# A planner that counts one more wait, and four pieces of work moved between queues, in a fused attention and gated-MLP block

## The chip, the cores and the metric

The kernel runs on one core of a Trainium2 chip. The metric is the device time of one execution in microseconds. A core has five engines that run their own instruction streams in order and meet at semaphores: TensorE (PE, matrix products into PSUM banks), VectorE (DVE), ScalarE (ACT), GpSimd (POOL) and SyncE (SP). A transfer (DMA) is issued by an instruction in the stream of an engine; in this kernel nearly all are issued by SP.

## What is computed

The input is x with 2048 rows of 576 columns. It is normalised row by row, goes through a 32-head attention (heads of 18 columns) and through a gated MLP of width 4608, and the two results are combined.

```
xn = layernorm(x)
q, k, v = split(xn @ wqkv)                       # 32 heads of 18
s = softmax(q @ k.T * 18 ** -0.5) @ v @ wo       # all heads, then the projection
h = gelu(xn @ w_gate) * (xn @ w_up)              # 2048 x 4608
g = silu(h @ w_down)
out = x + s * g
```

## The kernel before

**Numbers.** All large products are made of float16 matrices with a high and a low half (`whi`, `wlo`; `evh`, `evl`; `hhi`, `hlo`), three products for one. Weights are scaled by powers of two that come from their largest element, so each weight tile goes through a preparation: load (`raw`, and `draw` for the rows of `w_down`), row maxima on DVE (`amax`), a round trip through DRAM that spreads the maximum to all partitions (`mxd`, `mb`, then `top` on DVE), small scale operations, and the splits (`split_hi` on ACT, `split_lo` on GpSimd). `prep` (L211) returns these steps as a list of pieces. A `Rest(n)` among them holds the rest of the list back until n microseconds of planned time have passed.

**Stages.** First comes the layer norm, sixteen row tiles (`ln_scale` on DVE, `ln_hi` on ACT, `ln_lo` on GpSimd, transposes on PE), with q and k of the first six heads. Then, while PE works on v and on the q and k of the other heads in four groups j = 1 to 4, pair 0's score maxima begin. The results of a group leave PSUM by `evac_j` (L561): ACT writes the high half `evh`, DVE the low half `evl`, and `store` writes them to the DRAM tiles `QD[j]` and `KD[j]`, in six transfers for each block of 512 columns (four of `evh`, two of `evl`). `evh` and `evl` have three buffers each. Two rows of constants, `KD<-cst`, are added to each `KD[j]` by four transfers in `open_j` (L608).

**The main loop.** Attention runs over 16 pairs of heads. A step of it has a score product for the softmax (`qk2`, PE, then the exponential on ACT) and a score product of the next pair of heads for its row maxima (`qk1`, PE, then a `TENSOR_REDUCE` into `PM` on DVE). One PSUM tile each serves `qk1` and `qk2` here, so a step's products wait for the reduction and the exponential of the step before. Into a step go also slots of a gate/up product (two matrix products each, 27 slots to a unit) and stages D of the down projection. Two stages D make one output tile `y`; the first begins it in PSUM tile `md`, the second, called late, is followed on DVE by the addition into `y`, which frees `md`. A round is some six or seven steps, holds one gate/up unit, and ends with a closing step that has no slots but a burst: the products of the probabilities with v (L1498), into `md` or `ma`, then an addition into `osb` on DVE.

**What sets the order.** `make_plan` (L1701) chooses for each round how many steps it has, which of them hold a stage D and how many slots each one gets. It takes the cheapest by `lost` (L1680), a small model of PE, ACT and DVE with the constants of L1657 (slot 0.2158, stage D 0.735, the two score products 0.43, burst 2.9). In that model a stage D waits for the last addition into `y`; a burst does not. Other work (preparations, the softmax's normalisation, the gate's polynomial) is put between by `subtick` (L152) where the planned room of its engine allows.

**Around the end of a pair.** `max_end` (L1425) turns the row maxima into two extra rows of `QT`, in three parts a, b, c at three steps: a reduction (a), two small operations that make high and low halves `rmc` (b), a 32x32 transpose into `rms` and the transfers to DRAM and back into `QT` (c). All its arithmetic is on DVE. At the start of a pair `load_v` (L1406) loads its values `VT`.

Of the kernel before, what the change touches and what calls it, by code (L numbers as in the profile page):

```python
# [12 lines left out]
F32 = mybir.dt.float32  # L13
# [7 lines left out]
P = 128  # L21
# [74 lines left out]
def kernel(ctx: ExitStack, tc: tile.TileContext, x, wqkv, wo, w_gate, w_up, w_down, out):  # L96
# [114 lines left out]
    def prep(name, parts, n, down=None, urgent=False, free=None, dfree=None, lead=1, vec=(), spare=False, home=None, early=False, slow=1.0):  # L211
# [9 lines left out]
        def load():  # L221
            if spare:
                if spare == "P":
                    body = ap.tile([P, 2, 512], F32, tag="P", name=f"rawa_{name}", bufs=6)
                else:
                    body = wp.tile([P, 2, D], F32, tag="draw", name=f"rawa_{name}", bufs=1)
                body = body.rearrange("p a b -> p (a b)")[:, 0:8 * n].rearrange("p (t i n) -> p t i n", t=4, i=2)
                last = ap.tile([P, 512], F32, tag="osb", name=f"rawb_{name}", bufs=2)
                last = last[:, 0:2 * n].rearrange("p (i n) -> p i n", i=2)
            else:  # L230
                raw = wp.tile([P, 5, 2, n], F32, tag="raw", name=f"raw_{name}", bufs=1)
                body, last = raw[:, 0:4], raw[:, 4]
            w.raw = [body[:, t] for t in range(4)] + [last]
            (src, c0), (src1, c1) = parts
            rows = src.tensor.shape[1]
            if src1.tensor.name == src.tensor.name and c1 == c0 + n:
                cols = [(
                    [[1, 2 * n]], body.rearrange("p t i n -> p t (i n)"), last.rearrange("p i n -> p (i n)"), c0, src
                )]
            else:  # L240
                cols = [([[1, n]], body[:, :, i, :], last[:, i, :], c, t) for i, (t, c) in enumerate(parts)]
            for dims, dst, dst4, c, t in cols:
                q.dma_start(
                    dst,
                    bass.AP(tensor=t.tensor, offset=t.offset + c, ap=[[rows, P], [P * rows, 4]] + dims),
                )
                q.dma_start(
                    dst4,
                    bass.AP(
                        tensor=t.tensor, offset=t.offset + c + 512 * rows, ap=[[0, 2], [rows, 64]] + dims  # L250
                    ),
                )
# [147 lines left out]
        if early and down is not None:  # L400
            add(dload)
            rest(6.0)
        elif not early:
            rest(13.0)
        for t in range(5):
            add(lambda t=t: amax(t), dve)
        if down is not None:
# [153 lines left out]
    def evac_j(j, part, sb, mt, n, late=None):  # L561

        nh = n // DH
        ev = {}

        def hi():
            ev["h"] = wp.tile([P, 512], F16, tag="evh", name=f"evh_{j}_{part}_{sb}", bufs=3)
            nc.scalar.activation(ev["h"][0:n], mt.t[0:n], AF.Copy, scale=2.0 ** -22)
            mt.done()

        def lo():
            ev["l"] = wp.tile([P, 512], F16, tag="evl", name=f"evl_{j}_{part}_{sb}", bufs=3)
            nc.vector.scalar_tensor_tensor(  # L573
                ev["l"][0:n], mt.t[0:n], 2.0 ** -22, ev["h"][0:n], op0=ALU.mult, op1=ALU.subtract
            )
            mt.done()

        def store():
            cols = slice(512 * sb, 512 * sb + 512)
            if part == 0:  # L580
                rows = (("h", 0), ("h", DH), ("l", 2 * DH))
                dst = QD[j]
            else:
                rows = (("h", 0), ("l", DH), ("h", 2 * DH))
                dst = KD[j]
            q = nc.gpsimd if j == 0 and part == 0 and sb == NB - 1 else nc.sync
            for key, r in rows:
                q.dma_start(dst[0:nh, r:r + DH, cols], ev[key][0:n])
            jdone[j] = jdone.get(j, 0) + 1

        if late is None:
            t0 = defer.now
            defer.at(t0 + 1, hi)
            defer.at(t0 + 2, lo)
            defer.at(t0 + 3, store)
            return

        def both():
            hi()
            lo()  # L600
            defer.at(defer.now + 2, store)

        if late:
            defer.at(defer.now + 1, both, on_act())
        else:
            both()

    def open_j(w, j):  # L608
        nh = len(heads_of(j))
        QD[j] = dp.tile([7, 54, S], F16, tag=f"QD{j}", name=f"QD{j}")  # L610
        KD[j] = dp.tile([7, 56, S], F16, tag=f"KD{j}", name=f"KD{j}")
        for b in range(NB):
            nc.sync.dma_start(KD[j][0:nh, 54:56, 512 * b:512 * b + 512], cst[0:2 * nh, :])
# [691 lines left out]
    with tc.manual_schedule():  # L1305
# [51 lines left out]
        for it in range(2, NT + 2):  # L1357
            if it == 2:
                open_j(w0, 0)
                preps[0], pieces = prep(*order[0][1], urgent=True, vec=(0, 1, 2, 3, 4))  # L1360
                pv0 = deque(f for _, f in pieces)
                pv0.popleft()()
            if it == 4:
                pj1 = make_prep(1, spare=True, early=True)
                pj1.pop(0)[1]()
            if 5 < it + 2 < NT:
                ln_scale(it + 2)
            if 4 < it + 1 < NT:
                ln_hi(it + 1)
            if 4 <= it < NT:  # L1370
                ln_out(it)
            if 4 < it + 1 < NT:
                ln_lo(it + 1)
            stats((8, 8, 6, 6)[it - 2] if it < 6 else 5)
            subtick()
            proj_fine(it - 2)
            if it < 4:
                ln_tr(it)
                ln_out(it)
            if 3 <= it < NT - 1:  # L1380
# [44 lines left out]
    def max_end(p):  # L1425

        st = {}

        def a():
            mx = st["mx"] = sm.tile([P, 2, NT], F32, tag="rmx", name=f"rmx{p}", bufs=2)  # L1430
            nc.vector.tensor_reduce(mx, PM[p], op=ALU.max, axis=AX.X, negate=True)

        def b():
            mx = st["mx"]
            mc = st["mc"] = sm.tile([P, 2, 2, NT], F16, tag="rmc", name=f"rmc{p}", bufs=2)
            nc.vector.tensor_scalar(mc[:, :, 0], mx, 2.0 ** -15, None, op0=ALU.mult)
            nc.vector.scalar_tensor_tensor(
                mc[:, :, 1], mx, 2.0 ** -15, mc[:, :, 0], op0=ALU.mult, op1=ALU.subtract
            )

        def c():
            st["mt"] = sm.tile([P, 64], F16, tag="rms", name=f"rms{p}", bufs=1)
            nc.vector.transpose(st["mt"], st["mc"].rearrange("p a b c -> p (a b c)"))
# [160 lines left out]
        p.pop(0)[1]()  # L1604
    lj3, lj4 = pj3.pop(0), pj4.pop(0)
    bg.append(Rest(14.0))
    bg.extend(pj1 + pc0[:1] + [lj3] + pj2[:8] + pj3[:6] + pj2[9:13] + pj3[7:8] + pj2[13:])
    bg.extend([lj4] + pj3[9:] + pj4[:6] + pc0[2:5] + pj4[7:8] + pc0[5:9] + pj4[9:13] + pc0[9:10])
    bg.extend(pj4[13:19] + pc0[11:12] + pj4[19:] + [Rest(2.5)] + pc0[13:])
    fills(11, 2.0)  # L1610
# [69 lines left out]
    def lost(steps, exp):  # L1680
# [3 lines left out]
        for d, g, late, first in steps:  # L1684
# [117 lines left out]
    for p in range(NPAIR):  # L1802
# [3 lines left out]
        for i in range(4 * NT):  # L1806
            s, half = divmod(i, 2)
            qh, kt = divmod(s, NT)
            if more and 0 <= i - 64 + AHEAD < 3:
                if i == 64 - AHEAD:  # L1810
                    steps = max_end(p + 1)
                steps[i - 64 + AHEAD]()
# [171 lines left out]
```

## Time and profile before

| | us |
|---|---|
| median of three runs | 2555.39 |
| lowest and highest | 2551.89, 2556.73 |
| the profiled execution, device time | 2558.73 |
| its span, first to last instruction | 2556.9 |
| PE busy | 2474.2 |
| DVE busy | 1839.1 |
| ACT busy | 1651.4 |
| POOL busy | 1534.2 |

The span is the part of the execution that the trace shows; the rest of the device time, 1.8 us, lies around it. Busy times of different engines overlap. A PE that is called busy is not always at its peak, so the start-to-start distance of its products is read besides.

### The profile page before, as it was taken

Reading aid. Unit: us, or ns where it says so; the run is one execution under the profiler, and the core shown is the slowest. Engines: PE = TensorE matmul, PEld = TensorE weight load, DVE = VectorE, ACT = ScalarE, POOL = GpSimd, SP = SyncE. Lnnn points to the kernel's source line nnn. Section 1 sums busy time; section 2 is a strip of 40 time slices with the busy share of each in tenths; the row PEclk is TensorE's granted clock in tenths of the full one; section 3 lists DMA queues with packets and bytes.
Section 4 is the critical chain, followed back from the end, with each engine's and each line's share of the span. In section 5 each row is a group of like instructions: output and inputs, shape, how many; then the busy total and the mean of one; then the engine's idle time right before and its main releaser. Section 6 shows DMA issues by size and latency. Waiting matters only on the chain.

```text
span 2556.9 us, 61384 instructions
## 1 busy us (share of the span) xinstructions
PE 2474.2 (97%) x26216; PEld 1305.8 (51%) x26216; DVE 1839.1 (72%) x2134; ACT 1651.4 (65%) x2002; POOL 1534.2 (60%) x1543
## 2 busy tenths in 40 slices
PE   7998999999999999999999999999999999999998
PEld 6865545444444444444444444444444544444555
DVE  7475577877777777777777777777877777677644
ACT  6222567667676667676767666676666776766674
POOL 3343767576675757484747666666667566757423
PEclk9998999999999999999999999999999999999999
DMA  4633111120111011011111010111111101110124
GB/s 153 165 103 119 26 32 34 35 57 11 53 35 33 14 47 41 16 37 31 37 30 51 17 50 14 41 25 38 30 38 25 41 25 42 24 35 10 41 63 140
DMA packets 139748, 118.74 MB, mean 46 GB/s; under 512 B 64828, under 2 KB 118904, under 8 KB 139474
## 3 DMA queue, kind: packets, MB, share of 16 engines
q1 hardware_dynamic: 136610, 106.97, 15.5%
q0 software_dynamic: 1568, 5.32, 0.6%
q8 instruction: 207, 3.39, 0.5%
q10 hardware_dynamic: 1296, 2.51, 0.3%
q14 instruction: 67, 0.55, 0.1%
HBM read 84.89 MB, written 29.61 MB: 45 GB/s over the span
## 4 chain that ended last, share of the span: by engine, by line
PE 82%; DVE 12%; DMA 3%; issue 1%; POOL 1%; ACT 1%; SPq 0%; ACTq 0%; POOLq 0%; DVEq 0%
PE ma_t L518 17%; PE md_t L1498 17%; PE mb_t L518 14%; PE md_t L821 13%; PE s L1473 8%; PE s L1418 8%; DVE PM L1421 6%; DVE y L841 3%; PE ma_t L1498 1%; DMA KD<-evh 1%; DMA VT<-VS 1%; PE pv_t L518 1%; PE md_t L1003 1%; PE mb_t L1003 1%; PE ma_t L1003 1%
## 5 line engine op out<-in xcount | busy, mean ns | idle before, releaser
L1421 DVE TENSOR_REDUCE PM<-s 128x2 f32<-128x1024 f32 x1024 | 1251.7, 1223 | 350.1 <-PE s L1418 332.9
L1479 ACT ACTIVATE P<-s,etab 128x1024 f32<-128x1024 f32 x960 | 1067.6, 1114 | 591.9 <-PE s L1473 582.7
L518 PE MATMUL ma_t<-XHT,whi_c 64*128 64x512 f16 x1430 | 539.5, 377 | 1.2 <-DVE evl L573 1.2
L518 PE MATMUL mb_t<-XHT,whi_c 64*128 64x512 f16 x1430 | 539.3, 377 | 0.6 <-DVE evl L573 0.6
L518 PE MATMUL ma_t<-XHT,wlo_c 64*128 64x512 f16 x1287 | 485.2, 377 | 0.0
L1498 PE MATMUL md_t<-P,VT 128*32 128x512 f32 x3744 | 434.7, 596 | 26.4 <-DVE y L841 22.6
L518 PE MATMUL mb_t<-XHT,wlo_c 64*128 64x512 f16 x1144 | 431.4, 377 | 0.0
L518 PE MATMUL mb_t<-XL,whi_c 64*128 64x512 f16 x1144 | 431.2, 377 | 0.0
L518 PE MATMUL ma_t<-XL,whi_c 64*128 64x512 f16 x1144 | 431.1, 377 | 0.0
L1418 PE MATMUL s<-KT,QT 54*128 54x512 f16 x2048 | 394.4, 378 | 23.0 <-DVE PM L1421 23.0
L1473 PE MATMUL s<-QT,KT 56*128 56x512 f16 x2048 | 396.4, 379 | 0.5 <-ACT P L1479 0.4
L518 PEld LDWEIGHTS <-whi_c 64*128 64x128 f16 x5184 | 261.0, 94 | 243.4 <-issue 7.2
L782 POOL TENSOR_TENSOR hlo<-gv,hhi 128x512 f16<-128x512 f32 x144 | 167.6, 1164 | 290.0 <-ACT hhi L775 287.3
L821 PE MATMUL md_t<-dhi_c,hhi 64*128 64x288 f16 x2304 | 331.7, 283 | 0.8 <-DVE osb L1506 0.5
L821 PE MATMUL md_t<-dhi_c,hlo 64*128 64x288 f16 x2304 | 331.1, 282 | 0.0
L821 PE MATMUL md_t<-dlo_c,hhi 64*128 64x288 f16 x2304 | 330.5, 282 | 0.0
L757 POOL TENSOR_SCALAR tw<-tw 128x512 f32<-128x512 f32 x144 | 93.6, 650 | 354.8 <-ACT tw L749 354.3
L821 PEld LDWEIGHTS <-hhi 64*128 64x128 f16 x4608 | 228.4, 94 | 133.2 <-issue 4.1
L1498 PEld LDWEIGHTS md_t<-P,VT 128*32 128x32 f32 x3744 | 107.6, 109 | 279.7 <-issue 194.9
L1506 DVE TENSOR_TENSOR osb<-md_t,osb 128x512 f32<-128x512 f32 x138 | 95.4, 691 | 206.4 <-PE md_t L1498 206.1
L1473 PEld LDWEIGHTS <-KT 56*128 56x128 f16 x2048 | 119.8, 94 | 228.8 <-issue 129.0
L841 DVE SCALAR_TENSOR_TENSOR y<-md_t,c_c,y 128x576 f32<-128x576 f32 x272 | 219.9, 809 | 15.0 <-PE md_t L821 15.0
(255 smaller groups left out, 3976.3 us busy)
## 6 DMA issues: line engine op xcount, KB each, us to landing
draw_c<-in_B_w_down SPq DMA_DIRECT2D x18, 576.0 KB
raw_c<-in_B_w_gate SPq DMA_DIRECT2D x18, 512.0 KB
raw_c<-in_B_w_up SPq DMA_DIRECT2D x18, 512.0 KB
obr<-rd SPq DMA_DIRECT2D x30, 256.0 KB
KT<-KD SPq DMA_DIRECT2D x32, 224.0 KB
QT<-QD SPq DMA_DIRECT2D x32, 216.0 KB
VS<-vst POOLq DMA_DIRECT2D x16, 304.0 KB, 6.3
VT<-VS SPq DMA_DIRECT2D x16, 304.0 KB
```

Source lines behind the costliest of these rows:

```text
L518: m = nc.tensor.matmul(o, lw, xx, start=self.stage == 0 and self.k == 0, stop=self.stage == 1 and self.k == self.slots - 1, skip_group_che ...
L757: gp.tensor_scalar(st["t"], st["t"], 1.0, 1.0, op0=ALU.mult, op1=ALU.add)
L782: gp.tensor_tensor(hs.lo[:, ft], st["v"], hs.hi[:, ft], op=ALU.subtract)
L821: m = nc.tensor.matmul(self.t.t[:, hf, 0:288], a[r, ft, sl], b[r, ft, 288 * hf:288 * hf + 288], start=self.stage == 0 and k == 0, stop=sel ...
L841: nc.vector.scalar_tensor_tensor(yy, y, w.c, yy, op0=ALU.mult, op1=ALU.add)
L1003: m = nc.tensor.matmul(o, a, b, start=self.stage == 0 and self.k == 0, stop=self.stage == 1 and self.k == len(terms) - 1, skip_group_check ...
L1418: nc.tensor.matmul(s1[:, h], QT[p][r, P * qt:P * qt + P], KT[p][r, 512 * kb:512 * kb + 512], start=True, stop=True)
L1421: nc.vector.tensor_reduce(PM[p][:, :, qt, kb:kb + 1], s1, op=ALU.max, axis=AX.X)
L1473: nc.tensor.matmul(s2[:, h], KT[p][r, P * kt:P * kt + P], QT[p][r, 512 * qb:512 * qb + 512], start=True, stop=True)
L1479: nc.scalar.activation(pt, s2, AF.Exp, scale=ETAB[j0])
L1498: nc.tensor.matmul(t.t[qd:qd + 32, :], VT[p][:, c0:c0 + 32], pt[:, h], start=kt == k0, stop=kt == k1, skip_group_check=True,)
L1506: nc.vector.tensor_tensor(osum[p, qh], t.t, osum[p, qh], op=ALU.add)
```

## The change

It has five parts.

1. In `lost`, a closing step without a stage D now waits for the last addition into `y`, plus 0.055. No instruction is added; the plans that `make_plan` picks are other ones.
2. `max_end` has two parts instead of three. The two small operations go back to GpSimd, and a scaling that was inside both is an operation of its own, so there are three. They are issued with the reduction; the transpose follows two steps later, as before in the main loop.
3. In `store`, the transfers of `evh` for j of 1 and more are issued by ACT and not by SP. `evl` stays with SP.
4. The `KD<-cst` rows for j of 1 and more are written during the layer norm, two transfers in each of eight iterations, issued by GpSimd (`ones_of`).
5. In `prep`, the load `draw` of a main-loop unit's down weights comes 6.0 of planned time after the `raw` loads and not right behind them; the rest before the maxima is 13.0 in all as before. In the early list, a `Rest(3.0)` stands ahead of the third group's `top`.

```diff
@@ prep
-            if not early:
-                dload()
@@
         elif not early:
-            rest(13.0)
+            if down is not None:
+                rest(6.0)
+                add(dload)
+                rest(7.0)
+            else:
+                rest(13.0)
@@ evac_j, store
-                q.dma_start(dst[0:nh, r:r + DH, cols], ev[key][0:n])
+                (nc.scalar if j and key == "h" else q).dma_start(dst[0:nh, r:r + DH, cols], ev[key][0:n])
@@
+    def ones_of(j, b):
+
+        if b == 0:
+            spaces(j)
+        nh = len(heads_of(j))
+        nc.gpsimd.dma_start(KD[j][0:nh, 54:56, 512 * b:512 * b + 512], cst[0:2 * nh, :])
+
     def open_j(w, j):
...
-        for b in range(NB):
+        for b in range(0 if j else NB):
             nc.sync.dma_start(KD[j][0:nh, 54:56, 512 * b:512 * b + 512], cst[0:2 * nh, :])
@@ layer norm, iteration it
+            if 6 <= it < 14:
+                for b in (0, 2):
+                    ones_of(1 + (it - 6) // 2, b + it % 2)
@@ max_end
         def a():
-            mx = st["mx"] = sm.tile([P, 2, NT], F32, tag="rmx", name=f"rmx{p}", bufs=2)
+            gp = nc.gpsimd
+            defer.spend(on_pool(1.0))
...
             nc.vector.tensor_reduce(mx, PM[p], op=ALU.max, axis=AX.X, negate=True)
+            gp.tensor_scalar(mx, mx, 2.0 ** -15, None, op0=ALU.mult)
+            gp.tensor_scalar(mc[:, :, 0], mx, 1.0, None, op0=ALU.mult)
+            gp.tensor_tensor(mc[:, :, 1], mx, mc[:, :, 0], op=ALU.subtract)
 
         def b():
-            mx = st["mx"]
-            mc = st["mc"] = sm.tile([P, 2, 2, NT], F16, tag="rmc", name=f"rmc{p}", bufs=2)
-            nc.vector.tensor_scalar(mc[:, :, 0], mx, 2.0 ** -15, None, op0=ALU.mult)
-            nc.vector.scalar_tensor_tensor(
-                mc[:, :, 1], mx, 2.0 ** -15, mc[:, :, 0], op0=ALU.mult, op1=ALU.subtract
-            )
-
-        def c():
@@ early list
-    bg.extend(pj1 + pc0[:1] + [lj3] + pj2[:8] + pj3[:6] + pj2[9:13] + pj3[7:8] + pj2[13:])
+    bg.extend(pj1 + pc0[:1] + [lj3] + pj2[:8] + pj3[:6] + [Rest(3.0)] + pj2[9:13] + pj3[7:8] + pj2[13:])
@@ lost
             t += BURST if g is None else g * G_SLOT
+            if g is None and not d:
+                t = max(t, y + 0.055)
```

(In the file the two added lines of `lost` stand ahead of the line that adds the burst.)

What the first part does to a common round is best seen on DVE, in pair 2 of the main loop; `PM` is a step's reduction, `y` the addition that ends two stages D, `osb` the addition that ends a burst. Before:

```order
L1421 TENSOR_REDUCE PM_7722<-s_3_46_9520 128x2
L1421 TENSOR_REDUCE PM_7722<-s_3_47_9553 128x2
L1421 TENSOR_REDUCE PM_7722<-s_3_48_9581 128x2
L841 SCALAR_TENSOR_TENSOR y<-md_t,c_c_7741,y 128x576
L1421 TENSOR_REDUCE PM_7722<-s_3_49_9614 128x2
L1421 TENSOR_REDUCE PM_7722<-s_3_50_9641 128x2
L1421 TENSOR_REDUCE PM_7722<-s_3_51_9671 128x2
L841 SCALAR_TENSOR_TENSOR y<-md_t,c_c_7741,y 128x576
L1421 TENSOR_REDUCE PM_7722<-s_3_52_9709 128x2
L1552 TENSOR_TENSOR osb_0_8425<-osb_0_8425,obr_0_9598 128x512
L1506 TENSOR_TENSOR osb_1_9513<-md_t,osb_1_9513 128x512
```

The second `y` stands one reduction ahead of the burst's `osb`. The same round now:

```order
L1438 TENSOR_REDUCE PM_7724<-s_3_46_9523 128x2
L1438 TENSOR_REDUCE PM_7724<-s_3_47_9563 128x2
L855 SCALAR_TENSOR_TENSOR y<-md_t,c_c_7743,y 128x576
L1438 TENSOR_REDUCE PM_7724<-s_3_48_9594 128x2
L1438 TENSOR_REDUCE PM_7724<-s_3_49_9617 128x2
L1438 TENSOR_REDUCE PM_7724<-s_3_50_9649 128x2
L855 SCALAR_TENSOR_TENSOR y<-md_t,c_c_7743,y 128x576
L1438 TENSOR_REDUCE PM_7724<-s_3_51_9687 128x2
L1438 TENSOR_REDUCE PM_7724<-s_3_52_9710 128x2
L1567 TENSOR_TENSOR osb_0_8427<-osb_0_8427,obr_0_9598 128x512
L1521 TENSOR_TENSOR osb_1_9516<-md_t,osb_1_9516 128x512
```

Both `y` stand one step earlier, so that two reductions lie between the last `y` and the burst. On PE the round was: 7 slots; D, 3; D, 4; 7; D, 3; D, 3; burst. It is now: 4 slots, D; D, 4; 6; D, 3; D, 4; 6; burst. This shape replaces the other in every round that had it; rounds that had D, D, none, none, D, D, burst now have D, D, none, D, D, none, burst.

The second place is SP's queue where group 1 of q and k ends and group 2 begins. Before:

```order
L588 DMA KD_2265<-evh_1_3_2629 6x18x512
L588 DMA KD_2265<-evl_1_3_2631 6x18x512
L588 DMA KD_2265<-evh_1_3_2629 6x18x512
L307 DMA mb_j_2645<-mxd_j_2556 128x128
L613 DMA KD_2649<-cst 6x2x512 x4
L588 DMA QD_2264<-evh_0_3_2633 6x18x512 x2
L588 DMA QD_2264<-evl_0_3_2635 6x18x512
L588 DMA KD_2649<-evh_1_0_2722 6x18x512
L588 DMA KD_2649<-evl_1_0_2724 6x18x512
L588 DMA KD_2649<-evh_1_0_2722 6x18x512
```

Now SP has there the following rows, which reach further on:

```order
L591 DMA KD_492<-evl_1_3_2649 6x18x512
L305 DMA mb_j_2663<-mxd_j_2574 128x128
L591 DMA QD_491<-evl_0_3_2653 6x18x512
L591 DMA KD_610<-evl_1_0_2736 6x18x512
L591 DMA QD_609<-evl_0_0_2740 6x18x512
```

and ACT has the other stores, each pair behind the two operations that write `evh`:

```order
L571 ACTIVATE evh_1_3_2647<-mc_t 108x512
L571 ACTIVATE evh_0_3_2651<-pv_t 108x512
L591 DMA KD_492<-evh_1_3_2647 6x18x512 x2
L591 DMA QD_491<-evh_0_3_2651 6x18x512 x2
L571 ACTIVATE evh_1_0_2734<-ma_t 108x512
L571 ACTIVATE evh_0_0_2738<-mb_t 108x512
```

The constants are gone from SP here, and of a block's six stores two are left on it.

The third place is GpSimd at the end of pair 2's maxima, which before had no operation of `max_end`; `tw` and `gv` are the gate's polynomial. Before:

```order
L740 TENSOR_TENSOR tw_3_0_9972<-gs_3_0_9926 128x512
L741 TENSOR_SCALAR tw_3_0_9972<-tw_3_0_9972 128x512
L742 TENSOR_TENSOR tw_3_0_9972<-tw_3_0_9972,gs_3_0_9926 128x512
L743 TENSOR_TENSOR gv_3_0_9938<-gv_3_0_9938,gs_3_0_9926 128x512
L757 TENSOR_SCALAR tw_3_0_9972<-tw_3_0_9972 128x512
```

Now:

```order
L756 TENSOR_TENSOR tw_3_0_9974<-tw_3_0_9974,gs_3_0_9919 128x512
L757 TENSOR_TENSOR gv_3_0_9933<-gv_3_0_9933,gs_3_0_9919 128x512
L1452 TENSOR_SCALAR rmx_10085<-rmx_10085 128x32
L1453 TENSOR_SCALAR rmc_10086<-rmx_10085 128x2x16
L1454 TENSOR_TENSOR rmc_10086<-rmx_10085,rmc_10086 128x2x16
L771 TENSOR_SCALAR tw_3_0_9974<-tw_3_0_9974 128x512
```

The three small operations stand behind the four operations of a gate's polynomial. At the start of pair 7, on SP, `draw` stood ahead of `VT<-VS` and now stands behind it; the four `raw` loads stand ahead of it in both.

More of the change, by code (lines that the diff above doesn't have):

```diff
@@ L606, in evac_j, with spaces @@
             both()
+    def spaces(j):
+        QD[j] = dp.tile([7, 54, S], F16, tag=f"QD{j}", name=f"QD{j}")
+        KD[j] = dp.tile([7, 56, S], F16, tag=f"KD{j}", name=f"KD{j}")
+    def ones_of(j, b):
[3 more added lines that the diff above has]
+        nc.gpsimd.dma_start(KD[j][0:nh, 54:56, 512 * b:512 * b + 512], cst[0:2 * nh, :])
     def open_j(w, j):
         nh = len(heads_of(j))
-        QD[j] = dp.tile([7, 54, S], F16, tag=f"QD{j}", name=f"QD{j}")
-        KD[j] = dp.tile([7, 56, S], F16, tag=f"KD{j}", name=f"KD{j}")
-        for b in range(NB):
+        if j not in QD:
+            spaces(j)
+        for b in range(0 if j else NB):
             nc.sync.dma_start(KD[j][0:nh, 54:56, 512 * b:512 * b + 512], cst[0:2 * nh, :])
@@ L1429, in a @@
         def a():
-            mx = st["mx"] = sm.tile([P, 2, NT], F32, tag="rmx", name=f"rmx{p}", bufs=2)
+            gp = nc.gpsimd
+            defer.spend(on_pool(1.0))
+            mx = sm.tile([P, 2, NT], F32, tag="rmx", name=f"rmx{p}", bufs=2)
+            mc = st["mc"] = sm.tile([P, 2, 2, NT], F16, tag="rmc", name=f"rmc{p}", bufs=2)
             nc.vector.tensor_reduce(mx, PM[p], op=ALU.max, axis=AX.X, negate=True)
+            gp.tensor_scalar(mx, mx, 2.0 ** -15, None, op0=ALU.mult)
+            gp.tensor_scalar(mc[:, :, 0], mx, 1.0, None, op0=ALU.mult)
+            gp.tensor_tensor(mc[:, :, 1], mx, mc[:, :, 0], op=ALU.subtract)
         def b():
-            mx = st["mx"]
-            mc = st["mc"] = sm.tile([P, 2, 2, NT], F16, tag="rmc", name=f"rmc{p}", bufs=2)
-            nc.vector.tensor_scalar(mc[:, :, 0], mx, 2.0 ** -15, None, op0=ALU.mult)
-            nc.vector.scalar_tensor_tensor(
-                mc[:, :, 1], mx, 2.0 ** -15, mc[:, :, 0], op0=ALU.mult, op1=ALU.subtract
-            )
-        def c():
             st["mt"] = sm.tile([P, 64], F16, tag="rms", name=f"rms{p}", bufs=1)
@@ L1808 @@
             qh, kt = divmod(s, NT)
[L1809 to L1812, printed above, removed]
+            if more and i == 64 - AHEAD:
+                steps = max_end(p + 1)
+                steps[0]()
+            if more and i == 66 - AHEAD:
+                steps[1]()
             if p == NPAIR - 2:
```

4 lines of the change are left out of this document (2 added, 2 removed).

## The prediction

> **What bounds the kernel now.** I read the page's head first, then PE's waits, in the first 300 us and from 300 to 2400 apart, then busy time and clock by stage.
>
> ```profile
> span 2556.9 us, 61384 instructions
> PE 2474.2 (97%) x26216; PEld 1305.8 (51%) x26216; DVE 1839.1 (72%) x2134; ACT 1651.4 (65%) x2002; POOL 1534.2 (60%) x1543
> ...
> PE s L1418 <- DVE PM L1421: 17.2, 4, 10.1
> ...
> PE md_t L1498 <- DVE y L841: 22.4, 99, 0.3
> PE s L1418 <- DVE PM L1421: 5.8, 8, 1.8
> PE ma_t L1498 <- DMA VT<-VS: 4.4, 2, 4.1
> ```
>
> The columns of a wait are: total us, times, longest. PE is the bound at 97%, so only time in which PE waits or runs slowly can be won, some 83 us in all. The first of these rows belongs to the first 300 us, the other three to the main loop. The biggest is a tiny wait, 0.23 us, that comes 99 times: a burst waits for the addition into `y`. The windows show where else time is lost (window, its us, busy us and instructions of PE, PEld, DVE, ACT, POOL, then PE's granted clock, DMA share, GB/s):
>
> ```profile
> 100.00:300.00 200.00, 179.91 (x1701) 118.91 (x1699) 122.45 (x159) 56.43 (x99) 89.07 (x109) 0.93 0.35 96
> 300.00:1280.00 980.00, 965.52 (x10072) 479.96 (x10070) 741.10 (x806) 675.62 (x770) 647.18 (x640) 1.00 0.13 34
> 1280.00:1300.00 20.00, 15.63 (x152) 7.23 (x150) 11.89 (x13) 8.73 (x11) 7.16 (x7) 0.91 0.23 55
> 110.00:125.00 15.00, 11.46 (x144) 9.09 (x141) 8.38 (x12) 4.18 (x13) 4.41 (x11) 0.89 0.76 142
> 157.00:172.00 15.00, 11.49 (x84) 7.01 (x82) 9.39 (x17) 3.60 (x8) 1.30 (x3) 0.77 0.39 94
> 222.00:245.00 23.00, 12.88 (x96) 6.72 (x92) 7.54 (x9) 3.41 (x5) 2.81 (x3) 0.70 0.35 118
> 250.00:270.00 20.00, 17.35 (x136) 9.66 (x134) 11.83 (x21) 3.50 (x6) 8.34 (x11) 0.91 0.36 99
> ```
>
> From 100 to 300 us PE idles for 20 us, nearly all of it in four stalls, and behind each of them its granted clock is down. So a stall costs twice: its idle time, and what PE then loses at a lower clock, (1 - clock) x window. For the four it is 3.5 + 1.7, 3.5 + 3.5, 10.1 + 6.9 and 2.7 + 1.8, together 33.7 us.
>
> **Part 1, the plan.** Here is a burst (L1498) that waits and, from another round, one that does not, on PE, with a DVE reduction of the second round and the `y` and reduction of the first.
>
> ```profile
> 668.05 0.38 PE L1418 MATMUL s<-KT,QT 54*128 54x512 f16 x2
> 668.66 0.64 PE L1498 MATMUL md_t<-P,VT 128*32 128x512 f32 x4 [0.23 <-DVE y L841]
> ...
> 622.65 0.38 PE L1418 MATMUL s<-KT,QT 54*128 54x512 f16 x2
> 622.96 0.64 PE L1498 MATMUL md_t<-P,VT 128*32 128x512 f32 x4
> ...
> 623.07 1.23 DVE L1421 TENSOR_REDUCE PM<-s 128x2 f32<-128x1024 f32 x1 [0.94 <-PE s L1418]
> 667.80 0.81 DVE L841 SCALAR_TENSOR_TENSOR y<-md_t,c_c,y 128x576 f32<-128x576 f32 x1
> 668.52 1.22 DVE L1421 TENSOR_REDUCE PM<-s 128x2 f32<-128x1024 f32 x1
> ```
>
> From the score product to the burst it is 0.61 us with the wait and 0.31 without, although the idle time is put at 0.23, since the ends of products are modelled. `y` runs to 668.61, when PE has been ready for 0.3. In the new rounds the last `y` stands one step and one reduction (1.22) earlier, so the wait is gone: 99 x 0.30 = 29.7 us, at least 99 x 0.23 = 22.4 if I trust only the idle time. No instruction is added on any engine.
>
> What is late next? PE's step without a stage D has two score products and six slots now, 0.43 + 6 x 0.216 = 1.73 us. DVE needs 0.42 from a score product to its reduction (622.65 to 623.07), 1.22 for that, then 0.81 for `y`, then 1.22 for the next reduction and 0.06 (the planner's constant) to release PE: 3.73 us for two steps. PE takes 0.43 + 0.74 + 4 x 0.216 = 2.03 for the one with the stage D and 1.73 for the other, 3.76. DVE just keeps up, by 0.03 us; before, a step of seven slots left 0.25. An additional DVE operation next to a `y` will therefore show on PE. Most of these stand in the closing step, beside a burst. I give back 2 us: **28 us**, with 0 and 30 as the ends.
>
> **Part 2, the maxima.** The place is `max_end` of a pair.
>
> ```profile
> 839.84 1.18 DVE L1436 TENSOR_SCALAR rmc<-rmx 128x32 f16<-128x32 f32 x1
> 841.05 0.97 DVE L1437 SCALAR_TENSOR_TENSOR rmc<-rmx,rmc 128x32 f16<-128x32 f32 x1
> 843.09 0.23 DVE L1443 STREAM_TRANSPOSE rms<-rmc 128x64 f16<-128x64 f16 x1
> ...
> L1437 DVE SCALAR_TENSOR_TENSOR rmc<-rmx,rmc x16: 191/193/1203, 264.5 to 2409.3; 128x32 f16<-128x32 f32 x16
> L330 POOL TENSOR_SCALAR E_c<-E_c x18: 216/225/237, 181.5 to 2191.1; 128x2 f32<-128x2 f32 x18
> ...
> 979.83 0.29 DVE L1431 TENSOR_REDUCE rmx<-PM 128x32 f32<-128x128 f32 x1
> 982.74 1.26 POOL L743 TENSOR_TENSOR gv<-gv,gs 128x512 f32<-128x512 f32 x1
> ```
>
> The fifth row's columns are min, median and max in ns. The two small operations should take 0.2 us each; here they take 1.18 and 0.97, and that holds up the reductions behind them. They go, and with them up to the 5.8 us that PE waited for `PM` in the main loop, the most there is to win here. Added are three GpSimd operations a pair, bounded by the smallest on GpSimd, 0.22, with gaps some 0.3 each, so 0.9 a pair or 14 us in all on an engine that is 60% busy. They hide beside PE unless the transpose, two steps (3.5 us) later, gets to wait for them; queued behind it on DVE are the reductions, and PE waits for those. In the case shown the gate's polynomial ends on GpSimd at 984.0, the three would end at 984.9, and the transpose would be due near 980.1 + 3.5 = 983.6: it waits 1.3 us. The four operations of the polynomial stand there for most pairs, but mostly earlier. I take 4 us won, from 5.8 down to minus 6 (16 pairs with a PE wait of 0.4).
>
> **Part 3, the queues of the early stage.** SP's instructions come here with what waited for them on ACT:
>
> ```profile
> 156.71 3.71 SPq L613 DMA_DIRECT2D KD<-cst  x4
> 159.09 0.60 ACT L568 ACTIVATE evh<-ma_t 108x512 f16<-108x512 f32 x1 [5.99 <-DMA KD<-cst]
> ...
> 219.13 1.61 SPq L247 DMA_DIRECT2D raw_c<-in_B_w_up  x1
> 220.84 2.68 SPq L259 DMA_DIRECT2D draw_c<-in_B_w_down  x1
> 223.62 0.82 SPq L588 DMA_DIRECT2D KD<-evh  x1
> 232.70 0.60 ACT L568 ACTIVATE evh<-pv_t 126x512 f16<-126x512 f32 x1 [10.44 <-DMA KD<-evh]
> ...
> 130.00:220.00 90.00, 86.45 (x764) 59.30 (x762) 64.56 (x85) 23.07 (x43) 39.85 (x49) 0.96 0.38 109
> 115.39 0.29 DVE L313 TENSOR_REDUCE mg_j<-mb_j 128x1 f32<-128x128 f32 x1 [3.31 <-DMA mb_j<-mxd_j]
> ```
>
> SP issues a store in some 0.8 us, six a block, and a block takes PE 27 slots, 5.8 us. So SP has nothing to spare, and when the constants (3.71) or a weight load come in, the stores are late, `evh` has no free buffer, DVE waits for ACT in order, and PE for DVE's reduction. With four stores of six on ACT and the constants gone, SP has 1.6 us a block. ACT gets 4 x 0.8 = 3.2 a block; it is busy for 23 of 90 us there, 1.5 a block, so it holds. The stall at 157 goes, 7.0 us. Of that at 222, 17.0, I take 13: the raw loads still stand on SP ahead of `evl`, only `draw` comes later. At 110 DVE waited 3.3 for `mb`, and `Rest(3.0)` is ahead of this operation now; the load wait before it stays, so half of 5.2, say 2.5. The stall at 250 has other causes: 0. Together **22.5 us**, from 33.7 to 0.
>
> The Trainium skill (DMA: Bandwidth & Descriptors, Issuing engines are not separate DMA queues) says that starting transfers from several engines only saves the time of the sequencer that starts them, as all run on the same DMA engines. By that rule part 3 would win nothing if the transfers were the limit; the DMA share of 0.38 in the row above says that they are not, and the SP rows that the sequencer is.
>
> **Part 4, constants during the layer norm.** Sixteen issues come into GpSimd's queue between the `xn` operations, two an iteration, and PE's transposes wait for these.
>
> ```profile
> 63.60 0.61 POOL L588 DMA_DIRECT2D QD<-evl  x1 [0.26 <-DVE evl L573]
> POOL xn L1271 <- ACT xn L1267: 28.8, 13, 7.4
> ```
>
> At 0.61 each it is 9.8 us, and GpSimd idles 28.8 us ahead of the `xn` operations, which covers most. I take 2 us lost; the ends are 0 and 9.8. The Trainium skill (SBUF — State Buffer, SBUF: two separate sides) speaks against this part: DVE and GpSimd share a port pair as an exclusive lock, and GpSimd cannot write a transfer's descriptors while DVE runs certain operations; the layer norm's scaling on DVE may be one. The `rmc` rows above, 0.19 us at the least and 1.2 at the most, look like such a lock; for transfers no row here shows it. By this rule the loss would tend to the 9.8.
>
> **Part 5, `draw` later.** At pair 7 PE waited for the values, with its half-clock stretch behind it (the window 1280 to 1300 above: 0.09 x 20 = 1.8).
>
> ```profile
> 1275.85 3.26 SPq L259 DMA_DIRECT2D draw_c<-in_B_w_down  x1
> 1279.16 0.67 SPq L1410 DMA_DIRECT2D VT<-VS  x1
> 1287.97 1.27 PE L1498 MATMUL ma_t<-P,VT 128*32 128x512 f32 x8 [4.14 <-DMA VT<-VS]
> ```
>
> `VT` moves past a large load whose issue alone takes 3.26; the raw loads stay ahead of it. 4.1 + 1.8 = 5.9 can go, I take 5; the ends are 5.9 and 0.
>
> **Sum.** 28 + 4 + 22.5 - 2 + 5 = 57.5 us. From the profiled execution's 2558.7 that gives 2501.2; its time lies 3.3 above the median of 2555.4, so the forecast is **2498**.
>
> **The rivals.** (a) The plan's gain is given back. The wait moves from `y` to the score products, because DVE has only 0.03 us left per pair of steps. For it: on average DVE is free a quarter of the time (741 of 980 us), but next to a `y` it is not. Against: rounds without the wait exist in this trace, as at 622. If each round loses 0.28 again, the time is 2498 + 28 = 2526.
> (b) The early stage wins nothing: ACT, which now issues stores, waits with them for transfers on their way and is late for `evh` instead of SP. For it: ACT runs in order, and a store behind the raw loads may have to wait for them. Against: ACT is 26% busy there. 2498 + 22.5 = 2520. With (a) and (b) both, 2549.
> (c) The change does less than it says: the burst's 0.3 is not due to `y`, but to the change from score products to bursts. Against it the burst at 622, which comes at 0.31. This would give the time of (a).
> (d) Slower: the transpose waits for GpSimd at every pair. GpSimd works through a polynomial (four operations), a gate's end (two) and a weight split (two) in order. If all eight were ahead, at 1.26 us as `gv` above, it would be 10.1 + 0.9 - 3.5 = 7.5 us of wait a pair; PE would idle nearly as long and lose some 3.5 more at the lower clock, as behind the stall at 157: 16 x 11 = 176. With part 2's 4 us not won either, that is 2498 + 4 + 176 = 2678. It decides from 53.5 / 16 = 3.3 us of PE's time a pair. Against it: 1.3 us in the case shown, and that with the polynomial alone ahead.
>
> **How the numbers follow.** Forecast 0.62, (a) and (c) 0.13, (b) 0.16, (a) with (b) 0.06, (d) 0.03. The range: all that can be won is 29.7 + 5.8 + 33.7 + 5.9 = 75, so 2480 is the floor, and 2484 allows for a little; above it reaches over (a) and (b) to 2528. A measurement of this kernel can tell 0.2%, 5 us, from no change. Faster by more than this are all cases but (d): 0.95; within it 0.02, slower 0.03.
>
> **What would show it.** Right: the waits of L1498's bursts for `y` fall from 99 to a few and score product to burst is 0.31; no `rmc` on DVE, and the transpose never waits more than 2 us; the clock stays at 1.00 from 125 to 245 us; no wait for `VT` above 1 us. Wrong: score products waiting for `PM` some hundred times (a); `evh` waiting for transfers at 150 to 240 as before, or ACT's stores blocked (b); a DVE transpose behind GpSimd with a low clock at each pair's end (d).

## The result, and the profile after

Over five runs each the changed kernel takes 2511.2 us (2510.5 to 2512.6), the kernel before 2556.2 (2551.9 to 2557.7): a ratio of 0.9827, with a 95% interval of 0.9813 to 0.9842. It is 45 us faster; the forecast was 57.5. The profiled execution, 2512.6 us, begins its page thus:

```profile
span 2510.2 us, 61378 instructions
...
PE 2462.1 (98%) x26216; PEld 1300.8 (52%) x26216; DVE 1830.9 (73%) x2102; ACT 1648.3 (66%) x2002; POOL 1548.7 (62%) x1607
```

PE's waits, in us, times and longest: the first row is of the first 300 us, the other two are of 300 to 2360, the main loop. The windows behind them have the columns of the forecast's.

```profile
PE s L1435 <- DVE PM L1438: 13.8, 5, 7.1
...
PE ma_t L1513 <- DMA VT<-VS: 2.9, 1, 2.9
PE s L1435 <- DVE PM L1438: 1.0, 2, 0.7
...
130.00:180.00 50.00, 44.88 (x382) 28.89 (x380) 34.75 (x51) 11.21 (x22) 17.99 (x28) 0.93 0.36 100
215.00:245.00 30.00, 22.90 (x188) 13.46 (x185) 15.63 (x18) 5.76 (x10) 6.00 (x6) 0.83 0.33 109
280.00:1250.00 970.00, 968.53 (x10162) 483.04 (x10158) 743.63 (x798) 681.53 (x779) 657.61 (x669) 1.00 0.13 33
1250.00:1280.00 30.00, 27.05 (x266) 12.19 (x262) 21.06 (x23) 16.70 (x20) 15.08 (x17) 0.94 0.28 76
1280.00:2360.00 1080.00, 1079.60 (x11312) 538.44 (x11308) 829.44 (x886) 764.77 (x926) 704.66 (x711) 1.00 0.12 31
```

In the main loop no burst waits for `y` any more, and outside 1250 to 1280 PE idles 1.9 us of 2050. The early stage still has its stalls: 5.1 us idle from 130 to 180 and 7.1 from 215 to 245, each with a clock below 1.00.

To place the gain I follow the exponentials on ACT (`P<-s`), of which both kernels have 960: the first one and the 881st, before and after.

```profile
282.25 1.11 ACT L1479 ACTIVATE P<-s,etab 128x1024 f32<-128x1024 f32 x1 [2.16 <-PE s L1473]
2385.30 1.11 ACT L1479 ACTIVATE P<-s,etab 128x1024 f32<-128x1024 f32 x1 [0.71 <-PE s L1473]
...
276.92 1.12 ACT L1494 ACTIVATE P<-s,etab 128x1024 f32<-128x1024 f32 x1 [2.16 <-PE s L1488]
2340.28 1.11 ACT L1494 ACTIVATE P<-s,etab 128x1024 f32<-128x1024 f32 x1 [0.92 <-PE s L1488]
```

The early stage ends 5.3 us sooner; the loop from the first to the 881st takes 2063.4 in place of 2103.1, 39.7 less; the end is 1.7 shorter. Together 46.7, the difference of the spans. So the loop gave more than the 37 forecast for it (28 + 4 + 5), and the early stage 5 in place of 20.5.

### The profile page after: what moved, and what is told of

It is laid out like the page before. It is cut to its first block, busy times and chain, and to the rows that moved or that the text cites. A ratio compares the mean times of both kernels' runs of the same rounds, so it can differ in the third digit from the quotient of the medians.

```text
span 2510.2 us, 61378 instructions
## 1 busy us (share of the span) xinstructions
PE 2462.1 (98%) x26216; PEld 1300.8 (52%) x26216; DVE 1830.9 (73%) x2102; ACT 1648.3 (66%) x2002; POOL 1548.7 (62%) x1607
## 4 chain that ended last, share of the span: by engine, by line
PE 91%; DMA 3%; DVE 3%; POOL 1%; ACT 1%; issue 1%; ACTq 0%; POOLq 0%; SPq 0%; DVEq 0%
PE ma_t L521 18%; PE md_t L835 17%; PE md_t L1513 17%; PE mb_t L521 15%; PE s L1488 9%; PE s L1435 9%; PE ma_t L1513 1%; DMA KD<-evl 1%; PE pv_t L521 1%; PE md_t L1017 1%; PE mc_t L521 1%; DMA KD<-evh 1%; PE mb_t L1017 1%; PE ma_t L1017 1%; DVE PM L1438 1%
## 5 line engine op out<-in xcount | busy, mean ns | idle before, releaser
L1488 PEld LDWEIGHTS <-KT 56*128 56x128 f16 x2048 | 129.4, 94 | 226.4 <-issue 130.2
```

Of the source, the lines that this page charges most:

```text
L1488: nc.tensor.matmul(s2[:, h], KT[p][r, P * kt:P * kt + P], QT[p][r, 512 * qb:512 * qb + 512], start=True, stop=True)
```

## The experiments

The twelve kernels have four to eleven timed runs each. The kernel before measured 2556 to 2564 in their four groups, so ratios are compared, and 0.001 is 2.6 us. "Loop" is the stretch from the first to the 881st exponential, "pair 7" that from the 432nd to the 464th, both worked out from the exponentials' starts.

| kernel | median us | ratio to before (95%) | first exp. at | loop | pair 7 |
|---|---|---|---|---|---|
| before | 2556.2 | | 282.3 | 2103.1 | 75.7 |
| changed | 2511.2 | 0.9827 (0.9813 to 0.9842) | 276.9 | 2063.4 | 73.4 |
| p1_plan | 2514.8 | 0.9835 (0.9821 to 0.9848) | 279.1 | 2064.8 | 68.8 |
| p2_maxima | 2552.1 | 0.9981 (0.9972 to 0.9990) | 277.1 | 2099.1 | 76.2 |
| p3_queues | 2552.1 | 0.9986 (0.9977 to 0.9995) | 277.1 | 2104.0 | 76.4 |
| p4_down | 2551.8 | 0.9982 (0.9974 to 0.9991) | 277.7 | 2099.8 | 72.4 |
| p5_plan_queues | 2516.7 | 0.9832 (0.9816 to 0.9848) | 277.6 | 2064.0 | 68.8 |
| x1_rows | 2500.7 | 0.9776 (0.9763 to 0.9789) | 266.7 | 2063.1 | 73.4 |
| x2_poolq | 2511.9 | 0.9825 (0.9812 to 0.9839) | 273.3 | 2063.9 | 73.3 |
| x3_values | 2508.3 | 0.9807 (0.9794 to 0.9821) | 280.2 | 2058.6 | 68.8 |
| x4_all | 2494.5 | 0.9754 (0.9740 to 0.9767) | 263.6 | 2058.5 | 68.8 |
| x5_portions | 2486.4 | 0.9713 (0.9700 to 0.9726) | 256.6 | 2057.3 | 68.8 |
| x7_rows_sp | 2502.5 | 0.9777 (0.9763 to 0.9790) | 268.3 | 2064.6 | 75.2 |
| x8_dummy | 2520.0 | 0.9832 (0.9819 to 0.9845) | 281.1 | 2063.0 | 73.3 |

The loop repeats to 1 or 2 us between kernels that share it (2063.0 to 2064.6 for changed, x1, x2, x7 and x8). The early stage does not: four profiles with the old queues (before, p1, p2, p4) reach the first exponential at 277.1 to 282.3, four with the new ones (changed, p3, p5, x3) at 276.9 to 280.2.

### Each part alone

**The plan (p1).** The two lines of `lost`, in the kernel before.

> The kernel before with the planner's two new lines alone. The forecast's size: 28 us faster, some 2528. My reading of the changed kernel's trace (its main loop gains 0.29 us a round and no burst waits for y): 31 to 33 us faster, 2523 to 2525, with the early stage unchanged. Rival (a), the gain is given back at the reductions: within 3 us of the time before, and some hundred waits of score products for PM.

It wins 42 us (0.9835), nearly as much as the whole change. The loop is 38.3 shorter; 6.9 of that lie in the stretch at pair 7 (75.7 - 68.8), which no theory had. SP's rows there, in p1 first, then in the changed kernel:

```profile
1239.61 0.55 SPq L247 DMA_DIRECT2D raw_c<-in_B_w_up  x1
1245.25 0.37 SPq L259 DMA_DIRECT2D draw_c<-in_B_w_down  x1
...
1255.64 0.57 SPq L1410 DMA_DIRECT2D VT<-VS  x1
...
1252.28 1.05 SPq L247 DMA_DIRECT2D raw_c<-in_B_w_up  x1
1253.43 3.01 SPq L1427 DMA_DIRECT2D VT<-VS  x1
1256.48 5.22 SPq L257 DMA_DIRECT2D draw_c<-in_B_w_down  x1
```

With the plan alone the weights of the next block go out 10 us and more ahead of `VT`, which then lands in time. In the changed kernel they stand right ahead of it again, and `VT` is late.

**The maxima (p2)**: `max_end` as in the change, and its callers.

> The kernel before with the maxima's small operations on GpSimd alone. The forecast's size: 4 us faster. My reading of the changed kernel's trace, where the main loop's waits for PM fall from 5.8 to 1.0 us: 5 us faster, 2551. Rival (d), the transpose waits for GpSimd: slower by 6 us or more, with DVE transposes waiting for rmc over 2 us.

Some 5 us faster (0.9981), the loop 4.0 shorter. PE's waits for `PM` in the loop fall to the first row, and in the changed kernel the transpose waits for GpSimd as the second row says:

```profile
PE s L1418 <- DVE PM L1421: 2.5, 6, 0.6
...
DVE rms L1458 <- POOL rmc L1454: 1.4, 1, 1.4
```

**The queues (p3)**: parts 3 and 4, with `Rest(3.0)`.

> The kernel before with the stores of the high halves on ScalarE's queue, the constants on GpSimd and the rest of 3.0 ahead of the maxima's load. The forecast's size (parts 3 and 4): 20.5 us faster, 2536, and no stall of PE from 125 to 245 us. My reading of the changed kernel's trace, where the 64th reduction comes 5.3 us earlier than before: 5 us faster, 2551, with PE waiting some 7 us for PM near 225 us as in the changed kernel. Rival (b) in full: within 2 us of the time before.

Some 4 us faster (0.9986, so 1 to 6); in the profiles the early stage ends where it also ends without the edit. PE's waits for `PM` in the first 300 us stay, at 15.8 against 17.2:

```profile
PE s L1432 <- DVE PM L1435: 15.8, 4, 8.3
```

**The down weights (p4)**: the later `draw` of part 5, without `Rest(3.0)`.

> The kernel before with the down weights loaded 6 of the planner's microseconds behind the raw loads, alone. The forecast's size: 5 us faster, and no wait for VT above 1 us at pair 7. My reading of the changed kernel's trace, where the values still land 2.9 us late behind the raw loads: 1 to 2 us faster, 2554 to 2555, with a wait for VT of some 3 us at pair 7.

Some 5 us faster (0.9982), of which 3.3 in pair 7's stretch, where the wait for `VT` falls from 4.1 to 2.4.

The four gains alone make 42 + 5 + 4 + 5 = 56; the whole change has 45. They overlap.

**Parts 1, 3 and 4 together (p5)**, with `Rest(3.0)`, to see where.

> The kernel before with the planner's lines and the early stage's queues (parts 1, 3 and 4), without the maxima on GpSimd and the later down weights (parts 2 and 5). My reading: with the planner's lines alone the raw weights of the block at pair 7 go out 17 us ahead of the values, and parts 2 and 5 each bring them back to stand right ahead of the values, which costs what they win: no wait for VT above 1 us here, and 2509 to 2513, as the whole change. Rival (each part wins what it won alone, whatever the others do): 9 us slower than the whole change, some 2520.

No wait for `VT` and 68.8 at pair 7, as in p1. The ratio, 0.9832, is that of the whole change; the median, 2516.7, lies above the range that I gave, in a group in which the kernel before was 4 us slower too (2560.3; 0.9832 of 2556.2 is 2513). In SP's program order the raw loads stand right ahead of pair 7's `VT` as soon as part 2 or part 5 joins the plan; that is read from the programs, and no run here has the plan with one of them alone. The changed kernel is 5 to 6 us shorter than p5 in the other rounds. I put that down to part 2, since part 5 alone changes nothing there (2027.5 us in p4, 2027.3 before). At pair 7 the two together give 4.6 back (73.4 - 68.8).

### What holds the early stage

In the changed kernel ACT issues two `QD` stores at 155.04 only, the second of them when `mxd` has landed (157.1, by the completion semaphores). Its next `evh`, behind them, has idled 8.4 us, which the profile puts down to an earlier `QD` store (the first two rows). The transfers themselves crawl there. On SP, `mb` is issued when `mxd`, the 128 maxima of a block, has landed (SP's rows: before, then changed):

```profile
155.04 2.83 ACTq L591 DMA_DIRECT2D QD<-evh  x2
158.00 0.60 ACT L571 ACTIVATE evh<-ma_t 108x512 f16<-108x512 f32 x1 [8.40 <-DMA QD<-evh]
...
148.83 0.36 SPq L292 DMA_DIRECT2D mxd_j<-mx_j  x1
156.30 0.35 SPq L307 DMA_DIRECT2D mb_j<-mxd_j  x1
...
146.96 0.36 SPq L290 DMA_DIRECT2D mxd_j<-mx_j  x1
157.21 0.35 SPq L305 DMA_DIRECT2D mb_j<-mxd_j  x1
```

A store of 512 bytes takes 7.5 and 10.2 us. It is made of 128 pieces of 4 bytes. By the completion semaphores, ACT's stores issued right before and after it (145.8 to 149.8) land 9 to 10 us later, the two ahead of them (144.0 and 144.7) in 3 to 4.

**The maxima as rows (x1).** DVE transposes them first, so that 4 pieces of 128 bytes are stored; `mb` and `top` read them in that order.

```diff
-            w.md = dp.tile([P, k], F32, tag="mxd", name=f"mxd_{name}", bufs=2)
-            nc.sync.dma_start(w.md, w.mx[:, 0:k])
+            mt = sm.tile([P, 32], F32, tag="mxt", name=f"mxt_{name}", bufs=2)
+            nc.vector.transpose(mt, mx32)
+            w.md = dp.tile([k, P], F32, tag="mxd", name=f"mxd_{name}", bufs=2)
+            for r in range(k):
+                nc.sync.dma_start(w.md[r].rearrange("(a b) -> a b", b=32), mt[r:P:32, :])
```

> The changed kernel, with the 128 maxima of a weight block transposed on DVE before they are stored (4 rows of 128 bytes in place of 128 pieces of 4 bytes); one DVE operation more a block. In the changed kernel the transfers around 103 to 107, 113 to 122 and 149 to 156 us crawl, each time some 2 us behind such a store, and ScalarE's stores issued at 146 to 151 us land after 9 to 10 us in place of 4 to 5. Theory S (the 4-byte pieces cause it): the stores land within 6 us there, PE's idle time from 130 to 180 us falls from 5.1 us to under 2 and its clock stays at 1.00, so 6 to 9 us faster than the changed kernel, some 2503 to 2505. Rival (something else slows the transfers there, as the loads of instructions that stand there too): within 2 us of the changed kernel, 2511, and the late landings stay.

**Rows without parts 3 and 4 (x7)**: x1's edit on the plan, the maxima and the later `draw` of part 5; SP issues all six stores and the constants again, and `Rest(3.0)` is gone too.

> x1 without part 3 and 4 of the change: the maxima stored as rows, but all six stores of a block and the constants on SyncE again. The forecast's mechanism (SyncE's 0.8 us an issue is what the early stage waits for): 15 to 20 us slower than x1's 2500.7, some 2516 to 2521, with PE waiting for PM at 157 and 222 us. Rival (the slow transfers behind the 4-byte pieces were it, and the issuing queue matters little): within 5 us of x1, 2501 to 2506.

**The small store back, for nothing (x8)**: x1 and, for the early blocks, a store that nothing reads.

```diff
+            if early:
+                dmy = dp.tile([P, 1], F32, tag="dmy", name=f"dmy_{name}", bufs=2)
+                nc.sync.dma_start(dmy, mx32[:, 0:1])
```

> x1, with the 4-byte store of the maxima put back as one more store into a spare tensor that nothing reads, for the five early weight blocks (their maxima still travel as rows). Theory S (the 4-byte pieces themselves slow the transfers behind them): ScalarE's and SyncE's stores after the store of block j4 land after 8 to 10 us again, PE loses 5 to 10 us between 110 and 180 us, and the time is 2506 to 2511. Rival (x1 gains because the maxima arrive sooner, or because the order on the engines has shifted): within 3 us of x1's 2500.7, and the stores land within 6 us.

PE from 130 to 180 us in x1, x7 and x8, then GB/s from 140 to 160 us in steps of 0.5 in the changed kernel, x1 and x8, then SP in x1 and x8, then ACT and DVE in x8:

```profile
130.00:180.00 50.00, 50.00 (x459) 34.76 (x456) 41.09 (x62) 14.47 (x26) 19.75 (x27) 1.00 0.37 109
130.00:180.00 50.00, 50.00 (x458) 34.42 (x456) 40.87 (x62) 13.82 (x26) 20.92 (x26) 1.00 0.34 105
130.00:180.00 50.00, 44.80 (x405) 29.68 (x401) 34.31 (x51) 11.17 (x23) 15.11 (x22) 1.00 0.39 94
...
GB/s 121 98 109 88 113 125 145 129 139 137 82 94 129 121 127 156 143 130 139 119 76 68 63 31 25 2 10 55 39 61 86 31 96 113 117 104 76 86 154 157
GB/s 129 119 119 166 141 113 129 142 123 70 20 61 111 113 111 94 103 83 109 128 134 145 139 96 90 135 111 119 86 82 111 98 109 113 129 111 77 55 102 91
GB/s 123 127 109 137 139 147 143 86 78 119 121 88 80 84 86 117 141 117 10 37 50 27 20 6 21 32 51 66 39 29 16 57 82 131 111 76 96 117 173 130
...
141.24 0.54 SPq L296 DMA_DIRECT2D mxd_j<-mxt_j  x1
146.05 0.58 SPq L311 DMA_DIRECT2D mb_j<-mxd_j  x1
...
145.52 0.36 SPq L294 DMA_DIRECT2D dmy_j<-mx  x1
145.97 0.73 SPq L299 DMA_DIRECT2D mxd_j<-mxt_j  x1
157.14 0.35 SPq L314 DMA_DIRECT2D mb_j<-mxd_j  x1
...
152.73 0.60 ACT L580 ACTIVATE evh<-pv_t 108x512 f16<-108x512 f32 x1 [3.62 <-DMA KD<-evh]
158.59 0.60 ACT L580 ACTIVATE evh<-ma_t 108x512 f16<-108x512 f32 x1 [5.26 <-DMA QD<-evh]
153.36 0.69 DVE L585 SCALAR_TENSOR_TENSOR evl<-pv_t,evh 108x512 f16<-108x512 f32 x1 [3.52 <-ACT evh L580]
```

In the changed kernel the rate falls to 2 to 86 GB/s for 6 us, some 3 us behind the small store. In x1 there is a dip of 1.5 us, PE is never idle from 130 to 180, and the time falls by 13 us (0.9776 against 0.9827), more than I gave. Adding the small store back, which nothing reads, brings the trough back and costs 0.0056, 14 us, also more than I gave: 0.9832 of 2556.2 is 2513. The maxima arrive late in x8 too (`mb` is issued at 157.14), but from 130 to 182 us neither DVE nor ACT waits for them: DVE waits for `evh`, and ACT for stores (the last three rows). Only GpSimd waits for what is made of them, 23.8 us, and in x1 19.7 without a stall of PE. By the completion semaphores, the stores that x8 issues in the 2.3 us ahead of the small one land in 8 to 12 us. So the pieces of 4 bytes slow the transfers around them, those already on their way too; it is not the late maxima that hold PE.

x7 has the same ratio as x1: with all stores on SP again PE is still never idle from 130 to 180. SP's issue time was not what the stall at 157 waited for. The Trainium skill (DMA: Bandwidth & Descriptors, Specifications) gives 512 bytes as the least transfer for line rate and says that below it the DMA engines read, modify and write. That speaks of the small transfer's own rate; these runs show that the other transfers pay, for 6 us. Blocks with down weights have two maxima a row, so the same 128 pieces have 8 bytes. At 164.8 and 248.8 us such stores land in 3.9 and 5.0 us in the changed kernel, and those of the kernel before in 6.1 and 4.1; the stores of 4-byte pieces take 7.5 to 10.9 in these two kernels, and the one that x8 puts at the first of these places takes 10.3. So the size of the pieces seems to matter far below 512 bytes too; an experiment on that alone was not run.

**Another queue for the raw loads (x2).** The stall at 222 is another matter. In the changed kernel SP, ACT and DVE have there:

```profile
215.66 4.76 SPq L591 DMA_DIRECT2D KD<-evl  x1
...
217.67 4.17 ACTq L591 DMA_DIRECT2D QD<-evh  x2
...
228.15 0.69 DVE L576 SCALAR_TENSOR_TENSOR evl<-pv_t,evh 126x512 f16<-126x512 f32 x1 [4.88 <-DMA KD<-evl]
```

The stores stand behind 1.3 MB of raw weights, and DVE has no buffer for `evl`. x2 moves the two large loads, 1 MB, to GpSimd's queue, so that they are not ahead of the stores on SP's.

```diff
-        q = nc.sync
+        q = nc.gpsimd if name == "c1" else nc.sync
...
-                q.dma_start(
-                    dst4,
...
+                nc.sync.dma_start(dst4, last4)
```

> The changed kernel, with the two large raw loads of weight block c1 (near 210 us, 0.5 MB each) on GpSimd's queue, so that SyncE's stores no longer stand behind them in its queue and no store's completion semaphore waits for them. Theory Q (the stall at 222 us comes from the order in the queue): the stores of that time land within 7 us, PE's 7.1 us of idle time and the half clock of 10.3 us behind it go, 8 to 12 us faster than the changed kernel, some 2499 to 2503. Rival (the transfers share the DMA engines and memory, whatever the queue): DVE waits for KD<-evl as before, within 2 us of 2511.

The time is that of the changed kernel (0.9825). DVE still waits for the store, 6.1 us:

```profile
224.66 0.69 DVE L574 SCALAR_TENSOR_TENSOR evl<-pv_t,evh 126x512 f16<-126x512 f32 x1 [6.13 <-DMA KD<-evl]
```

So 1 MB less in SP's queue wins nothing. By the completion semaphores the stores of both queues take 7 to 12 us there, also ACT's, which have no load ahead of them in their queue. Theory Q falls for the large loads. Two small ones (0.13 MB each) still stand in SP's queue ahead of the store that DVE waits for, so the order there may be a part of it; no run here separates that.

**The values early (x3)**

```diff
+            if i == 40 and more:
+                load_v(p + 1)
```

> The changed kernel, with the values of the next pair loaded at step 40 of a pair in place of its start. My reading: the 2.9 us wait for VT at pair 7 and the 1.7 us of half clock behind it go, 4.6 us faster than the changed kernel, some 2506 to 2507, and no wait for VT anywhere. Rival (the load, moved, delays another transfer on SyncE, as the sums' way through memory): no gain, 2511, and another wait near a pair's start.

The loop is 4.8 us shorter and no wait for `VT` is left; the time falls by 5 us (0.9807), though the early stage of this profile ends late (280.2).

```profile
1250.00:1280.00 30.00, 30.00 (x320) 14.91 (x317) 24.94 (x28) 20.40 (x23) 19.47 (x20) 1.00 0.22 67
```

**Three together (x4)**

> The three edits of x1, x2 and x3 together on the changed kernel. If all three readings hold, their gains add: 19 to 26 us faster than the changed kernel, 2485 to 2492. If only the values' load counts: 2506 to 2507.

0.0073 below the changed kernel, 19 us: what x1 and x3 give, and nothing from x2.

**The raw loads in portions (x5)**: rows, early values, and c1's raw weights one fifth at a time.

```diff
+            if name == "c1":
+                for k in range(5):
+                    add(lambda k=k: portion(k))
+                    rest(3.0)
+                add(dload)
+                rest(4.0)
```

> The changed kernel with the maxima stored as rows (x1), the values loaded early (x3), and weight block c1's raw weights (1.3 MB) loaded in five portions, 3 of the planner's microseconds apart, in place of at once; its maxima are taken 6 us later. Theory W (the stores stand behind the bytes ahead of them on engines that all queues share): the stores near 210 to 230 us land within 7 us, the stall there (7.5 us of idle time and 10.2 us at half clock in x1) falls below 3 us, and the time is 8 to 11 us below x4's 2494.5, some 2484 to 2487. Rival (the bytes are the same and the stall is only spread out, or it moves to the end of block j4): within 3 us of 2494.5.

PE from 180 to 215 and from 215 to 245 us, in x1 and then in x5:

```profile
180.00:215.00 35.00, 32.10 (x294) 22.52 (x291) 19.82 (x22) 6.97 (x12) 14.93 (x15) 1.00 0.49 147
215.00:245.00 30.00, 24.68 (x194) 14.32 (x195) 19.96 (x25) 6.79 (x10) 12.42 (x16) 0.83 0.29 82
...
180.00:215.00 35.00, 35.00 (x322) 24.21 (x322) 24.26 (x26) 7.25 (x12) 15.39 (x16) 1.00 0.47 140
215.00:245.00 30.00, 27.41 (x228) 16.22 (x226) 19.38 (x26) 8.40 (x13) 15.22 (x18) 0.94 0.38 110
```

The idle time falls from 8.2 to 2.6 us, and the time by another 0.0041 against x4, 10 us, as theory W forecast. By the completion semaphores the stores issued from 203 to 214 us land in 3.5 to 7.5 us, in x1 in 6 to 12. How much of this is shared engines and how much the order in SP's queue is not shown, since the portions also let SP's own stores through between them. x5, at 2486.4 us, is the best version here, 74 us faster than the kernel before in its group and 29 us (0.0114) ahead of the changed one.

## Why the prediction was right, and where it was not

**Part 1**, taken as 28 of at most 30: 31.4 in the loop outside pair 7's stretch (p1: 38.3 - 6.9). The price of 0.30 was right and the count was short, since four more bursts wait for a `y` of another line in the trace of before:

```profile
PE md_t L1498 <- DVE y L839: 0.9, 4, 0.2
```

103 x 0.30 = 31. Some 1 us of the 31.4 is another wait, that for `PM` (4.7 in p1, 5.8 before), so the two agree to about 1 us. The 2 us that "I give back" for DVE did not come: in the loop of the changed kernel PE waits for `PM` twice. Rivals (a) and (c) fall. Unforeseen was that a plan also moves the weight loads against the pairs' starts, worth another 6.9 alone.

**Part 2**, 4: 4.0 in p2's loop. On top of the plan and outside pair 7's stretch it is 5 to 6: the changed kernel has 2063.4 - 73.4 = 1990.0 there, p1 1996.0 and p5 1995.2 (that it is part 2 and not part 5 is argued from p4, above). Rival (d) falls, with two waits of the transpose, 3.0 us in all.

**Part 3**, 22.5, is the step that failed: "So SP has nothing to spare, and when the constants (3.71) or a weight load come in, the stores are late". p3 shows 1 to 6 us for parts 3 and 4 with `Rest(3.0)`, and x7 against x1 nothing. What I read as SP's issue time was its wait. In the rows above, SP issues the constants at 156.71 in the trace of before because it sat behind `mb` until 156.30, and `mb` behind the slow `mxd`. The 7.0 of the stall at 157 stayed in another shape (from 130 to 180, 5.1 idle and 0.07 x 50 = 3.5 for the clock). Of the 17.0 at 222, of which I took 13, the changed kernel still pays 7.1 idle and 0.17 x 30 = 5.1 for the clock: the raw loads ahead of the stores, which I named, were most of it, for with the loads in portions x5 pays 2.6 + 1.8. At 110, taken as 2.5, PE idles 1.6 from 100 to 130 with its clock at 1.00 (before 3.5 and 0.94); but p2, without the edit, has 2.6 and 1.00, so this may be scatter. Rival (b) came true in its mechanism: ACT's stores wait for transfers on their way. The rule of the Trainium skill that I weighed (DMA: Bandwidth & Descriptors, Issuing engines are not separate DMA queues) decided rightly against part 3. My reason against it, a DMA share of 0.38, does not hold: the share is a mean over 90 us, and the trough that counted lasts 6 us with transfers on their way.

**Part 4**, 2 lost: PE's busy time in the first 100 us is 83.6 with it and 83.8 without (in p3 84.5, in p1 84.0), so nothing clear of the scatter; the loss that the lock would bring is not seen.

**Part 5**, 5: alone 3.3 in the loop (4.6 by the ratio). With the plan there was nothing left to win at pair 7 (68.8 in p1), and the changed kernel has 73.4. The step "the raw loads stay ahead of it" was right and was the point: 2.9 us of wait stayed, with half clock behind it.

So the sum, 57.5, is 11 above the profiled gain of 46.7: parts 3 and 4 gave 5.3 in place of 20.5 (and part of that is scatter of the early stage), parts 1, 2 and 5 gave 39.7 in place of 37, and the end 1.7. The time lies within the range because the range reached over rival (b), not because part 3 worked. Of the signs of being right two came true (no burst waits for `y`; the transpose waits at most 1.7 us), and two did not: the clock is 0.93 from 130 to 180 us and 0.83 from 215 to 245, and PE waits 2.9 us for `VT`.

## What to carry to other kernels

An instruction queue that looks full may only be waiting in order for one slow transfer: look for what the first late entry waits for before counting issue times. Keep 4-byte pieces out of stores to memory where other transfers are urgent, and send a large load in portions when small stores share its engines. A planner's new costs also move everything that is paced by its clock, so gains of single parts, measured alone, need not add.

## What the runs showed that I had not expected

- A store of 128 pieces of 4 bytes can be followed by some 6 us in which the rate of all transfers falls from some 110 GB/s to 2 to 86. The changed kernel has four of them in the early stage. Storing all maxima as rows won 13 us; five such stores put back cost 14 (one of them stands where the changed kernel has pieces of 8 bytes). Why memory reacts so was not tried.
- The early stage of the same code ends up to 3.3 us apart in different profiles (before 282.3 and p1 279.1; changed 276.9 and x3 280.2). In the kernels without the small stores and with the raw loads at once it ends at 263.6 to 268.3.
- The half clock behind a stall lasts 3.4 us or a multiple (6.8, 10.2, 13.7) in the clock records of all these traces, but for the last one, which the end cuts off.
